# Window attention in blocks of 32 queries with 64x32 float32 score tiles, from the third batch on, before a two-layer feed-forward

## The chip, the cores and the metric

One core of a Trainium2 chip runs the whole program. The metric is the device time of one execution in microseconds (us), as the median of several runs.

## The reference

Eight batches, eight heads, 512 local and 32 global tokens, head dimension 64. Each local query sees the 32 global keys and the local keys at most 32 positions away; each global query sees all 544 keys. The attention output (4352 rows of 512) goes through a feed-forward with 2048 hidden units.

```python
s_g = scale * np.matmul(q_g, k_all.transpose(0, 1, 3, 2))
out_g = np.matmul(sm(s_g), v_all)
s_ll = scale * np.matmul(q_l, k_l.transpose(0, 1, 3, 2))
mask = np.abs(pos[:, None] - pos[None, :]) <= window          # window = 32
s_ll = np.where(mask, s_ll, -1000000000.0)
s_lg = scale * np.matmul(q_l, k_g.transpose(0, 1, 3, 2))
a_l = sm(np.concatenate([s_lg, s_ll], axis=-1))
out_l = np.matmul(a_l, np.concatenate([v_g, v_l], axis=2))
...
h = x @ w_in                                                  # x: 4352 x 512
g = h - np.tanh(h)
return (g @ w_out).astype(np.float32)
```

## The kernel before

**The work.** Heads go in pairs, `Pair(j)`: pairs 0 to 7 are batches 1 and 2, pairs 8 to 31 are batches 3 to 8. A chunk is the feed-forward of one batch. It has 16 steps; a step is 12 hidden matmuls (`add_hidden`, L1521, 128x512) and 12 output matmuls (`add_out`, L1569, 128x512), because weights and activations are each split in a high and a low part (type float32r) and three of the four products are taken. The last batch's chunk and the global rows go through `Tail` (L1914, L1940, L2034).

**Attention of a pair from the third batch on** (`split_attention`): the global scores (L1340, 4 matmuls), and then, for each half `tp` of the 512 queries, scores of two tiles of 128 queries against 224 keys each (`scores`, L1150, float32r, three passes, 12 matmuls for two heads), mask and row maximum on DVE (L1459), exponential on ACT (L1466), scaling on POOL (L1229), 16 transposes of the probabilities back on TensorE (`transposes`, L1171), copies to SBUF, and the product with the values (`add_product`, L1248, float32, 8 matmuls). The first two batches have the same steps with float32 scores (`attention`).

A "visit" (`add_visit`) is a row of such matmul groups that TensorE does without anything between them; it takes all its PSUM banks at its start. A pair has two of them, transposes with the next half's scores (`add_both`), with the products placed on their own.

**PSUM.** Eight banks: attention and hidden matmuls share banks 0 to 3 (`"att"`, `"h"`), the output accumulators take 4 to 7 (`"acc"`). A hidden bank comes free when ACT has taken the tanh (L1529) and DVE the difference (L1532).

**Order.** The order of all instructions is written by a planner in the kernel (`Order.run`) before the program is built: of the operations whose inputs it reckons ready, it takes the one that can start first, and among those that start within `tol` of each other the one with the lowest `due`. `NUDGE` adds a number to the `due` of single operations, `CHOICE` moves single operations between engines. Both are lists of about two thousand and one thousand numbers, found for this very kernel; they begin at operation 214, which is behind the first batch's first steps, and do not touch the tail.

## Time and profile before

| | |
|---|---|
| median of 3 runs | 970.85 us (970.6 to 971.48) |
| the profiled execution | 971.94 us, of which 970.0 us lie between the first and the last instruction (the span) |
| busy: TensorE (PE) | 953.3 us, 98% of the span |
| busy: VectorE (DVE), ScalarE (ACT), GpSimd (POOL) | 645.5, 480.6, 370.7 us |
| granted TensorE clock | 1.000 of 2.4 GHz over the span |
| chain that ended last | PE for 91% of the span |

The table says which engine is filled and that the chain of work that ends last runs on it nearly all the time. A busy time of PE counts a matmul until its modelled end, which overlaps the next matmul; what a group of matmuls costs is read from the start of the group to the start of what follows it. A float32 matmul stands as two records in the trace, a float32r matmul and a transpose as one.

### The profile page before, as it was taken

The numbers are of one execution on the slowest core, as the hardware profiler recorded it, in microseconds if no ns is written. First come the engines' busy times: TensorE is split into PE (matmuls) and PEld (weight loads), VectorE is DVE, ScalarE is ACT, GpSimd is POOL, SyncE is SP. The second block draws the span as 40 slices with busy tenths as digits, with TensorE's granted clock in tenths as the row PEclk, the third lists the DMA queues.
The fourth block names the chain that finished last, engine by engine and source line by source line (L and its number), as shares of the span: only waits on it lengthen the run. The fifth ranks groups of instructions, "written<-read, shape, count | busy, mean of one in ns | idle before, by whom it ended". The sixth has DMA issues, their size and how long they took to land.

```text
span 970.0 us, 18571 instructions
## 1 busy us (share of the span) xinstructions
PE 953.3 (98%) x6411; PEld 782.7 (81%) x6411; DVE 645.5 (67%) x2029; ACT 480.6 (50%) x1332; POOL 370.7 (38%) x512
## 2 busy tenths in 40 slices
PE   7889999999999999999999999999999999999998
PEld 5677777888888888888888888888888888889986
DVE  6997768777666665766666667667635544798773
ACT  6976566646455434563355445534535434433232
POOL 4666756534444532425325343433332343101000
PEclk9999999999999999999999999999999999999999
DMA  8665344322223121321123122221212200100001
GB/s 220 159 180 163 86 118 112 88 39 42 44 47 83 31 41 26 69 65 23 34 39 83 31 41 40 50 71 35 41 20 72 40 2 16 44 1 1 1 1 66
DMA packets 195166, 57.32 MB, mean 59 GB/s; under 512 B 179712, under 2 KB 188416, under 8 KB 195072
## 3 DMA queue, kind: packets, MB, share of 16 engines
q1 hardware_dynamic: 193728, 55.61, 24.3%
q8 instruction: 51, 0.84, 0.4%
q10 hardware_dynamic: 1344, 0.52, 0.2%
q14 instruction: 43, 0.35, 0.1%
HBM read 47.19 MB, written 8.91 MB: 58 GB/s over the span
## 4 chain that ended last, share of the span: by engine, by line
PE 91%; DVE 3%; DMA 1%; POOL 1%; SPq 1%; issue 1%; ACT 1%; ACTq 0%; DVEq 0%; POOLq 0%
PE bank L1569 32%; PE bank L1521 32%; PE bank L1248 6%; PE bank L1914 6%; PE bank L2034 5%; PE bank L1150 4%; PE bank L1171 4%; PE bank L1340 1%; PE bank L1940 1%; DMA wpair<-in_moe_w_out_dram 1%; SPq L1031 0%; POOL prob L1229 0%; DMA stage<-in_moe_w_out_dram 0%; DVE pg L1085 0%; PE bank L1047 0%
## 5 line engine op out<-in xcount | busy, mean ns | idle before, releaser
L1538 POOL TENSOR_TENSOR glo<-t,ghi 128x512 fp32r<-128x512 f32 x89 | 116.6, 1311 | 221.2 <-PE bank L1569 79.6
L1529 ACT ACTIVATE t<-bank 128x512 f32<-128x512 f32 x112 | 66.9, 598 | 199.4 <-PE bank L1521 188.8
L1229 POOL TENSOR_SCALAR prob<-prob,st 128x224 f32<-128x224 f32 x240 | 107.8, 466 | 143.6 <-DVE st L1223 120.1
L1532 DVE TENSOR_TENSOR t<-bank,t 128x512 f32<-128x512 f32 x112 | 77.3, 691 | 124.7 <-ACT t L1529 124.2
L1569 PE MATMUL bank<-w_out_hi,ghi 128*128 128x512 f32 x448 | 125.8, 395 | 0.0
L1569 PE MATMUL bank<-w_out_hi,glo 128*128 128x512 f32 x448 | 124.7, 392 | 0.0
L1569 PE MATMUL bank<-w_out_lo,ghi 128*128 128x512 f32 x448 | 124.5, 392 | 0.0
L1459 DVE CUSTOM_DVE_ANT_0 prob<-bank,mask 128x224 f32<-128x224 f32 x240 | 80.8, 387 | 63.5 <-PE bank L1150 55.9
L1521 PE MATMUL bank<-x_hi,w_in_hi 128*128 128x512 f32 x448 | 123.0, 397 | 0.0
L1466 ACT ACTIVATE prob<-prob,st 128x224 f32<-128x224 f32 x240 | 113.2, 476 | 14.5 <-DVE st L1459 13.3
L1521 PE MATMUL bank<-x_lo,w_in_hi 128*128 128x512 f32 x448 | 120.2, 390 | 0.0
L1521 PE MATMUL bank<-x_hi,w_in_lo 128*128 128x512 f32 x448 | 119.1, 390 | 0.0
L870 ACT COPY keys_first<-bank 128x512 f32<-128x512 f32 (+2 forms) x150 | 69.9, 516 | 87.2 <-PE bank L1171 86.8
L1521 PEld LDWEIGHTS bank<-x_hi,w_in_hi 128*128 128x128 f32 x448 | 81.6, 188 | 21.6 <-issue 3.2
L1521 PEld LDWEIGHTS bank<-x_lo,w_in_hi 128*128 128x128 f32 x448 | 83.8, 188 | 17.7
L1569 PEld LDWEIGHTS bank<-w_out_lo,ghi 128*128 128x128 f32 x448 | 83.0, 188 | 18.4 <-issue 1.0
L1569 PEld LDWEIGHTS bank<-w_out_hi,glo 128*128 128x128 f32 x448 | 83.0, 188 | 18.2 <-issue 0.7
L1521 PEld LDWEIGHTS bank<-x_hi,w_in_lo 128*128 128x128 f32 x448 | 83.6, 188 | 17.3
L1569 PEld LDWEIGHTS bank<-w_out_hi,ghi 128*128 128x128 f32 x448 | 82.3, 188 | 18.7 <-issue 1.4
L1248 PE MATMUL bank<-keys_first,values 128*64 128x160 f32 (+3 forms) x1024 | 68.5, 276 | 4.1 <-ACT keys_first L870 2.9
L1248 PEld LDWEIGHTS bank<-keys_first,values 96*64 96x64 f32 (+1 forms) x1024 | 56.2, 136 | 11.8 <-ACT keys_first L870 6.2
L1382 DVE STREAM_TRANSPOSE gt<-pg 32x128 f32<-32x128 f32 x192 | 53.0, 276 | 10.3 <-POOL pg L1361 4.5
(260 smaller groups left out, 1596.4 us busy)
## 6 DMA issues: line engine op xcount, KB each, us to landing
values<-in_v_l_dram SPq DMA_DIRECT2D x128, 72.0 KB, 2.4
out_dram<-wpair SPq DMA_DIRECT2D x28, 256.0 KB, 2.1
rawkq<-in_k_l_dram SPq DMA_DIRECT2D x96, 64.0 KB, 2.3
rawkq<-in_q_l_dram SPq DMA_DIRECT2D x96, 64.0 KB, 2.3
values<-in_v_g_dram SPq DMA_DIRECT2D x64, 48.0 KB, 2.1
first_q<-in_moe_w_in_dram SPq DMA_DIRECT2D x6, 512.0 KB, 4.4
stage<-in_moe_w_out_dram SPq DMA_DIRECT2D x6, 512.0 KB, 4.6
stage<-in_moe_w_in_dram SPq DMA_DIRECT2D x6, 512.0 KB, 4.4
```

Source lines behind the costliest of these rows:

```text
L870: (nc.scalar.copy if e == "A" else nc.vector.tensor_copy)(dst, src)
L1229: nc.gpsimd.tensor_scalar(x, x, st[:, c:c + 1], 1.0, op0=ALU.mult, op1=ALU.mult)
L1248: nc.tensor.matmul(box["o"][h.e:h.e + D, o0:o0 + c1 - c0], values[:k, h.two, t + t // 2 + a], keys_first[:k, h.two, pair, a, c0:c1], start ...
L1382: nc.vector.transpose(gt[r, :c], view(src, [(P, c), (1, 32)], 32 * q))
L1459: nc.vector.tensor_tensor_reduce(out=self.pt(2 * tp + i)[:, :KC], in0=getattr(self, f"s_{tp}")[:, i, :KC], in1=masks[2 * tp + i], scale=-0 ...
L1466: nc.scalar.activation(x, x, AF.Exp, bias=col[:, c0 + i:c0 + i + 1], scale=-1.0, accum_out=col[:, 8 + tp + c0 + i:9 + tp + c0 + i])
L1521: nc.tensor.matmul(self.h[s][:, j * n:(j + 1) * n], w[:, cc, f * P:(f + 1) * P], self.x()[xi][:, cc, :n], start=part == 0 and cc == 0 and ...
L1529: nc.scalar.activation(tt_[q], self.h[s], AF.Tanh)
L1532: nc.vector.tensor_sub(tt_[q], self.h.pop(s), tt_[q])
L1538: eng[e].tensor_sub(gg[q][1], tt_[q], f32(gg[q][0]))
L1569: nc.tensor.matmul(self.acc[tt], g[:, j * self.n + tt * P:j * self.n + (tt + 1) * P], low_out(f) if wi else high_out(f), start=s == 0 and ...
L1914: nc.tensor.matmul(self.hold(tt, tags), g(), low_out(f) if wi else high_out(f), start=first and k < len(tts), stop=last and k == len(mms) - 1)
```

## The change

From pair 8 on a pair is a `WindowPair`. Each block of 32 queries takes its own 96 local keys and the 32 global ones, so a head's scores are 16 blocks of 32x128, written as 64x32 tiles of the array: 64 contraction rows of one head, 32 columns of one block, two matmuls of 64 moving columns each, in float32 and without the split in parts. The global scores go the same way, in four groups of 32 columns. One visit holds all 64 local and 16 global score matmuls of the pair. The second visit holds the products of the pair before (14 matmuls for each half) and then this pair's 16 transposes. The values are loaded once for each window of 96 keys (14 windows a head). Masks are made anew on POOL for the blocks. `NUDGE` and `CHOICE` are empty; the planner's other numbers stay. The first two batches and the tail keep their code.

```diff
-    NUDGE = {214: 0.47, 215: 39.97, 216: 57.05, 217: 55.56, 218: -51.2, 219: -791.25, 220: -863.76, 221: -648.08,
...
-    CHOICE = {220: {"D": 3.0}, 225: {"A": 1.0}, 226: {"P": 1.0, "D": 0.3}, 231: {"D": 0.3, "A": 1.0}, 237: {"D": 1.0},
...
+    NUDGE = {}
+    CHOICE = {}
...
+    class WindowPair:
+            self.at = base(2 * j) + CFG["win"]
...
+        def scores(self):
+            names = [("s", self.j, h) for h in range(2)]
+            kw, q, g = win_kw, win_q(), self.gcol
+            def mm(e, tags):
+                t_ = self.box["s"] = [bank([P, S], tags[n]) for n in names]
+                for t in range(NT):
+                    for last in range(2):
+                        for i in range(4):
+                            b = 4 * t + i
+                            c = W * window(b) + 2 * W * last
+                            o = t * P + 2 * W * last
+                            for h, x in enumerate(t_):
+                                r = slice(64 * h, 64 * h + 64)
+                                keys = view(kw[r], [(g - c, 2), (1, W)], c) if last else kw[r, c:c + 2 * W]
+                                nc.tensor.matmul(x[W * i:W * i + W, o:o + 2 * W], q[r, W * b:W * b + W], keys,
+                                                 start=True, stop=True, tile_position=(64 * h, W * i), skip_group_check=True)
...
+        def global_scores(self):
+                for x_, n, dims in ((0, 4 * W, [(6 * W, 2), (3 * W, 2), (1, W)]), (1, 2 * W, None)):
+                    for c in range(4):
+                        for h, x in enumerate(t_):
...
+                            nc.tensor.matmul(out, q[r], keys, start=True, stop=True, tile_position=(64 * h, W * c),
+                                             skip_group_check=True)
...
+            def peak(h, tp):
+                def fn(e, _):
+                    for t in (2 * tp, 2 * tp + 1):
+                        c = slice(t * P, t * P + P)
+                        nc.vector.tensor_tensor_reduce(out=self.prob[h][:, c], in0=self.box["s"][h][:, c], in1=win_mask(t), scale=-0.125,
+                                                       scalar=1e30, op0=ALU.add, op1=ALU.min, accum_out=s[:, 4 * h + t:4 * h + t + 1])
...
+        def product(self, half):
+                parts = [(1, 2 * G, 0, 3, W), (2, L + 64, G + 64, 1, 0), (3, L + 96, G + 96, 1, 0), (4, 0, 0, 2, L + 128),
+                         (5, L + 160, G + 160, 1, 0), (6, L + 192, G + 192, 1, 0), (7, G, 0, 2, L + 224 - G)]
...
+                for n, (b, c, o0, k, d) in enumerate(parts):
+                    for h in range(2):
...
+                        nc.tensor.matmul(dst, win_values[h][:, window(b)], src, start=n == 0, stop=n == len(parts) - 1, skip_group_check=True)
...
+        def add_values(self):
+                    nc.sync.dma_start(win_values[h][:96], bass.AP(v.tensor, v.offset, [[D, 96], [W * D, NB - 2], [1, D]]))
+                    nc.sync.dma_start(win_values[h][96:], bass.AP(g.tensor, g.offset, [[D, G], [0, NB - 2], [1, D]]))
...
-    pairs = [Pair(j) for j in range(NH // 2)]
+    pairs = [(Pair if j < H else WindowPair)(j) for j in range(NH // 2)]
...
+    def window_attention(j):
+        p.add_visit(p.at, [p.scores(), p.global_scores()])
+        p.add_softmaxes()
+        p.add_global_softmax()
+        p.add_visit(p.after(9.0), ([] if first else [last.product(0), last.product(1)]) + [p.transposes()])
+        if not first:
+            last.add_outputs()
+        p.add_turned()
+        p.add_values()
```

In `parts` the fourth number k is how many pieces of 32 moving columns a matmul takes: per half four matmuls with 32, two with 64 and one with 96 columns for each head.

On TensorE a pair from the middle of the program stood as follows before. `prob` are the probabilities that are turned, `kw` and `hi` the high parts of keys and queries, `w_out_hi` an output weight; "..." stands for rows of the same group.

```order
L1569 MATMUL bank_104<-w_out_lo,ghi_70 128x512
L1171 MATMUL bank_100<-idr,prob_96 128x64
...
L1150 MATMUL bank_103<-kw,hi_2057 128x224
L1150 MATMUL bank_102<-kw,hi_2057 128x224
...
L1150 MATMUL bank_102<-kw,wraw_2066 128x224
L1248 MATMUL bank_101<-keys_first,values 64x160 x2
L1248 MATMUL bank_101<-keys_first,values 64x96 x4
...
L1248 MATMUL bank_100<-keys_first,values 64x160 x2
L1521 MATMUL bank_102<-x_hi_108,w_in_hi 128x512 x4
```

With the change the same engine's order around one pair is this one: the score visit, feed-forward work, then the product and transpose visit, and feed-forward work up to the next score visit.

```order
L1234 MATMUL bank_102<-w_out_hi,ghi_72 128x512
L867 MATMUL bank_99<-first_m,hi_106 32x64
...
L889 MATMUL bank_101<-first_m,win_gq 32x2x64
...
L1234 MATMUL bank_105<-w_out_lo,ghi_72 128x512
...
L1186 MATMUL bank_99<-x_hi_87,w_in_hi 128x512 x4
...
L1047 MATMUL bank_100<-keys_first,values 64x96
...
L1011 MATMUL bank_99<-idr,prob 128x64
...
L1186 MATMUL bank_99<-x_hi_87,w_in_hi 128x512 x4
...
L867 MATMUL bank_101<-first_m,hi_106 32x64
```

What moved: three stops of TensorE in attention a pair (global scores, transposes with scores and products, transposes with scores) became two. Between the score visit and the next product visit stand 48 feed-forward matmuls at this place, 24 between that one and the next score visit.

On DVE, which frees the score banks and makes the row maxima, the order behind a score visit is now this one (`prob` are the masked scores, `st_93` the statistics, `t_69` a hidden tile, `first_m` the turned keys of the next pair).

```order
L1197 TENSOR_TENSOR t_69<-bank_99,t_69 128x512
L967 ISA prob,st_93<-bank_98,wraw_2020 128x128
...
L901 ISA pg,st_93<-bank_101,wraw_2020 128x192
...
L368 CAST ghi_72<-t_69 128x512
L908 COPY st_93<-st_93 32x2 x3
L918 TENSOR_REDUCE st_93<-st_93 32x2
...
L842 STREAM_TRANSPOSE first_m<-rawkq 128x512
L1197 TENSOR_TENSOR t_68<-bank_98,t_68 128x512
```

Here the eight maxima of both heads and the two of the global scores stand in one piece behind one visit; before, four maxima of 224 columns stood behind each of two visits, and the global ones on their own.

## Rows read from the trace of the kernel before

**Rows 1.** The page: busy us, share and instructions by engine; granted clock in 40 slices.

```profile
PE 953.3 (98%) x6411; PEld 782.7 (81%) x6411; DVE 645.5 (67%) x2029; ACT 480.6 (50%) x1332; POOL 370.7 (38%) x512
...
PEclk9999999999999999999999999999999999999999
```

**Rows 2.** Waits of PE from 60 us to the end: us, times, longest.

```profile
PE bank L1248 <- ACT keys_first L870: 0.3, 1, 0.3
PE bank L1171 <- POOL prob L1229: 0.2, 1, 0.2
```

**Rows 3.** Timeline of PE, one pair of the fifth batch: start, us, group, count.

```profile
502.63 0.42 PE L1340 MATMUL bank<-kw,gq 128*128 128x256 f32 x2
...
503.15 1.08 PE L1521 MATMUL bank<-x_hi,w_in_lo 128*128 128x512 f32 x4
...
508.70 0.69 PE L1171 MATMUL bank<-idr,prob 64*128 64x64 f32 x16
509.20 0.35 PE L1150 MATMUL bank<-kw,hi 64*128 64x224 f32 x2
...
510.12 2.05 PE L1248 MATMUL bank<-keys_first,values 128*64 128x160 f32 x32
512.09 1.20 PE L1521 MATMUL bank<-x_hi,w_in_hi 128*128 128x512 f32 x4
513.12 1.07 PE L1521 MATMUL bank<-x_lo,w_in_hi 128*128 128x512 f32 x4
...
517.66 0.39 PE L1569 MATMUL bank<-w_out_hi,glo 128*128 128x512 f32 x1
517.98 0.69 PE L1171 MATMUL bank<-idr,prob 64*128 64x64 f32 x16
...
519.31 0.50 PE L1569 MATMUL bank<-w_out_hi,ghi 128*128 128x512 f32 x1
519.65 0.40 PE L1569 MATMUL bank<-w_out_lo,ghi 128*128 128x512 f32 x1
```

**Rows 4.** Timeline of PE, eight output matmuls ahead of a visit in the sixth batch.

```profile
667.88 1.07 PE L1569 MATMUL bank<-w_out_hi,glo 128*128 128x512 f32 x4
668.79 1.07 PE L1569 MATMUL bank<-w_out_hi,ghi 128*128 128x512 f32 x4
669.79 0.69 PE L1171 MATMUL bank<-idr,prob 64*128 64x64 f32 x16
```

**Rows 5.** Timeline of PE, float32 matmuls of the second batch (each two records).

```profile
93.54 1.03 PE L1150 MATMUL bank<-first_kw,first_q 64*128 64x224 f32 x8
94.50 0.50 PE L1569 MATMUL bank<-w_out_hi,ghi 128*128 128x512 f32 x1
...
150.89 0.59 PE L1080 MATMUL bank<-first_kw,first_m 128*64 128x256 f32 x2
151.32 0.43 PE L1081 MATMUL bank<-first_kw,first_m 128*64 128x320 f32 x1
```

**Rows 6.** Timeline of PE and list of tile idr, 508.69 to 508.76 us: two first transposes.

```profile
508.70 0.28 PE L1171 MATMUL bank<-idr,prob 64*128 64x64 f32 x2
...
L1171 PE MATMUL bank<-idr,prob x2: 272/272/273, 508.7 to 508.7; 64*128 64x64 f32 x2
```

**Rows 7.** Groups of DVE, ACT, POOL, 250 to 850 us: busy us, mean ns, idle before.

```profile
L1532 DVE TENSOR_TENSOR t<-bank,t 128x512 f32<-128x512 f32 x86 | 59.3, 691 | 103.8 <-ACT t L1529 103.4
L1459 DVE CUSTOM_DVE_ANT_0 prob<-bank,mask 128x224 f32<-128x224 f32 x166 | 55.9, 387 | 54.2 <-PE bank L1150 46.8 <-POOL glo L1538 7.2
...
L1466 ACT ACTIVATE prob<-prob,st 128x224 f32<-128x224 f32 x166 | 78.3, 474 | 12.5 <-DVE st L1459 11.4
L1529 ACT ACTIVATE t<-bank 128x512 f32<-128x512 f32 x86 | 51.4, 598 | 171.9 <-PE bank L1521 163.0 <-POOL prob L1229 8.7
...
L1229 POOL TENSOR_SCALAR prob<-prob,st 128x224 f32<-128x224 f32 x168 | 74.9, 464 | 112.8 <-DVE st L1223 109.9 <-ACT x_hi L870 2.5 <-DVE kw L870 0.4
```

**Rows 8.** The page: DMA issues of local values, KB each, median us to landing.

```profile
values<-in_v_l_dram SPq DMA_DIRECT2D x128, 72.0 KB, 2.4
```

More of the change, by code (lines that the diff above doesn't have):

```diff
@@ L18 @@
 D = 64
+W = 32
 KC = 224
@@ L33, with __init__ @@
 class Later:
-    def __init__(self, pool, shape, tag):
-        self.make = lambda: pool.tile(shape, F32R, name=tag, tag=tag)
+    def __init__(self, pool, shape, tag, dt=F32R):
+        self.make = lambda: pool.tile(shape, dt, name=tag, tag=tag)
         self.tile = None
@@ L80, in add @@
                 before[id(x)] = x
+        if glue is not None:
+            before[id(glue)] = glue
         for x in before.values():
@@ L258 @@
     keys_first = cp.tile([P, 2, 2, 2, 384], F32, name="keys_first", tag="kf")
-    values = cp.tile([P, 2, 6, D], F32, name="values")
+    win_values = cp.tile([P, 960], F32, name="values")
+    values = win_values[:, :12 * D].rearrange("p (a t d) -> p a t d", a=2, d=D)
     SETS = [[f"{n}{u}" for n in ("rk", "rq", "pw", "pk", "pq")] for u in range(2)] + [["raw", "kq", "kw0", "kg0", "hk0"]]
@@ L1688, in attention @@
             p.add_head_scores(tp)
-            if tp and j + 1 == H:
-                next_keys(j)
             p.add_transposes(tp)
             p.add_product(tp)
-    def next_keys(j):
-        if (j + 1) % (H // 2) == 0:
-            add_globals(pairs[j + 1].b)
-        pairs[j + 1].add_split()
-    def split_attention(j):
-        p, more = pairs[j], j + 1 < len(pairs)
-        if j == H:
-            p.add_keys()
-            p.add_head_scores(0)
-        p.add_split_global_scores()
-        for a in p.heads:
-            a.add_values()
-        for h in range(2):
-            p.add_split_global_transpose(h)
-        p.add_both(0, p)
-        if more:
-            next_keys(j)
-            pairs[j + 1].add_keys()
-            p.add_both(1, pairs[j + 1])
-        else:
-            p.add_transposes(1)
-        for tp in range(2):
-            p.add_product(tp)
+    def window_attention(j):
+        p, last = pairs[j], pairs[j - 1]
+        first = last.b < 2
+        if first:
+            add_window_masks()
+        if p.jj == 0:
+            add_globals(p.b)
+        p.add_load()
+        p.add_visit(p.at, [p.scores(), p.global_scores()])
[6 more added lines that the diff above has]
+        p.add_values()
+        for h in range(2):
+            p.add_global_transpose(h)
     chunk = None
@@ L1755 @@
         ffn_steps(chunk, NF, NF + 1)
+    p = pairs[-1]
+    p.add_visit(p.after(32.0), [p.product(0), p.product(1)])
+    p.add_outputs()
     ntail = len(order.ops)
@@ L2186 @@
     for i, x in NUDGE.items():
-        if i < ntail:
-            order.ops[i].due += x
+        order.ops[i].due += x
+    for i, x in HOLD.items():
+        order.ops[i].ready = x
     for i, x in CHOICE.items():
-        for e, pen in x.items() if i < ntail else ():
+        for e, pen in x.items():
             d, old = order.ops[i].eng[e]
```

412 lines of the change are left out of this document (260 added, 152 removed), and 527 rows, old and new, of tables (CHOICE, NUDGE).

## The prediction

> **What bounds the kernel now.** The page's busy shares come first: PE is busy for 98% of the span at the full granted clock (2.4 GHz), the next engine, DVE, for 67% [rows 1]. A busy share can hide waits, so PE's own waits are read next: from 60 us to the end it waited for others twice, 0.5 us in all [rows 2]. The reader is to see that after the first 60 us the time is a sum of PE's work and nothing else. A change that takes work off PE is worth that work, as long as it puts no wait in its place; work taken off DVE, ACT or POOL is worth nothing by itself. In the first 60 us, where PE does wait, the order is the same as before on PE, so I leave that stretch as it is.
>
> **What a pair costs PE now.** I read it from starts in the timeline, not from busy times, since those overlap [rows 3]. The global scores run from 502.63 to 503.15, 0.52 us. The large visit runs from 508.70 to 512.09, 3.39 us. A visit starts late: four feed-forward matmuls take 0.91 us, and from the last four to the visit there are 1.00, so 0.09 us pass [rows 4]. The first four behind it take 1.03 us instead of 0.91, another 0.12. The small visit runs from 517.98 to 519.31, 1.33 us, with 0.32 - 0.23 = 0.09 ahead of it and 0.34 - 0.23 = 0.11 behind it. Sum: 0.52 + 0.09 + 3.39 + 0.12 + 0.09 + 1.33 + 0.11 = 5.65 us a pair. Feed-forward matmuls, first batches and tail do the same work as before.
>
> **The prices of the new matmuls.** A float32 matmul of 256 columns is two records and took 151.32 - 150.89 = 0.43 us [rows 5]: 0.84 ns a column and record. A record of 64 columns is then 0.054 us, one of 128 is 0.107. Two 64-row tiles run side by side: the eight records of 224 columns from 93.54 take 0.96 us until the next group, where one after the other they would need 8 x 0.188 = 1.50, and in pairs 0.75, which leaves 0.21 for lead and end [rows 5]. No row shows eight tiles at once, and that is the open price of this change.
>
> *Score visit.* 64 matmuls are 128 records of 64 columns on eight tiles, 16 on each: 16 x 0.054 = 0.86. The 16 global ones give each tile a matmul of 128 and one of 64 columns: 2 x 0.107 + 2 x 0.054 = 0.32. So 1.18 us if all eight tiles work at once, and with two at a time (9.48 us of records, halved) 4.74. I take 1.18. The two nearest rows speak for it: two row tiles gain their whole factor [rows 5], and the first two transposes, on different tiles, took 0.28 us together where each alone took 0.272 [rows 6]; issue does not hold a second tile back. With 0.09 ahead and 0.21 for lead and end the visit costs 1.48.
>
> *Product visit.* The products now move 704 columns for each head, before 1024 (the counts of the code). The 16 float32 matmuls of before take 512.09 - 510.12 = 1.97 us; at 1.68 ns a column, with the two heads side by side, 1024 columns make 1.72, so 0.25 is lead. Now 704 make 1.18. Eight of a head's fourteen matmuls have only 32 columns, 0.027 a record by columns; whether a record can be that short no row shows. The 16 transposes, eight to each row tile, last 509.20 - 508.70 = 0.50 us, 0.062 each, though 64 columns in one pass would be 0.027 [rows 3]: short records are paced by something else, I think by loading weights. So I count those sixteen records at 0.054, which adds 0.43 (bounds 0 and 0.43, the nearest row says the upper one): 1.61 + 0.25 = 1.86. The transposes are 16 where there were 32: 0.50. With 0.09 and 0.12 around it the visit costs 2.57.
>
> **The sum.** 1.48 + 2.57 = 4.05 a pair, 1.60 less than 5.65. There are 24 such pairs: 38.4 us. The last pair's products stand alone and the first pair's product visit has none, which cancels.
>
> **What else moves, and its cover.** Peaks, exponentials and scaling of a pair now stand behind one visit. Ten maxima at 0.39 at most (they have 128 and 192 columns instead of 224), with the last exponential 0.47 behind, and four of the second head's scalings at 0.46 each, make 3.9 + 0.5 + 1.9 = 6.3 us [rows 7]; statistics and the feed-forward's own work on DVE and POOL come between, say 2 to 3 us more. The cover is what PE does from one visit to the next: 48 feed-forward matmuls at 0.227 are 10.9 us, and the products stand ahead of the transposes, 1.9 us more. So I cost the chain at nothing; without cover it would cost some 9 us a pair. Each visit takes four banks at its start, among them the bank of the hidden step just done, which needs tanh and difference, 0.60 + 0.69 [rows 7]. Ahead of it stand eight output matmuls, 1.81 us. Before, a visit behind exactly that row started 669.79 - 668.79 - 0.91 = 0.09 us late, the same as behind longer ones [rows 4]; nothing was waited for.
>
> The values grow from six to fourteen windows: a transfer of 72 KB landed in 2.4 us [rows 8], the new one has 344 KB. If landing grew with the bytes it would be 11.5 us; from one product visit to the next there are 72 feed-forward matmuls and a score visit, 17.8 us. Behind these loads on SyncE's queue stand the next keys and queries, which are wanted a whole pair later. The masks are built on POOL ahead of the third batch, when it is busy for less than half of the time. All this I cost at nothing.
>
> *Empty tables.* The numbers that had been found took every wait away [rows 2]. The planner alone places a visit as soon as it reckons it ready, and its errors then become waits of PE. Nothing in the profile gives their size; the floor is 0, and a late start as large as the one at each visit now, 0.09 us, is what I allow: 0.1 x 48 visits = 4.8 us. The sum against the profiled execution is 971.94 - 38.4 + 4.8 = 938.3; that execution lies 1.1 above the median of the runs, so the forecast is **937 us**.
>
> **The rivals.**
>
> *Two tiles at a time.* If column tiles do not overlap, the score matmuls cost 4.74 instead of 1.18. A pair then costs 7.61, 1.96 more than before, and 24 of them 47 us more: 971.94 + 47 + 4.8 - 1.1 = 1023. It decides from 2.78 us for the 80 matmuls, that is at fewer than 3.4 tiles at a time. For it: no row shows more than two. Against: the tiles of the products are column tiles of 64, and they do reach 1.97 us where one after the other they would need 3.4 [rows 3]. With four at a time (2.37) the gain is 0.41 a pair, 10 us: 966.
>
> *Records that start one at a time.* The transposes average 0.031 us a record; if that is the pace at which any record starts, 160 of them cost 4.96 instead of 1.18, 2.18 us a pair over before: 971.94 + 52 + 4.8 - 1.1 = 1028. Against it stands the pair that starts together [rows 6]. The Trainium skill, page "TensorE: Matmul & The Clock Gate", section "Wait — 56ns, not 53.3ns?", has such a rule: starts are never closer than about 25 ns, however few columns. By it, as an estimate from that page, 160 records would cost 4.0 us and the kernel end near 1005 us. By that rule two records cannot lie within the 0.28 us row as they do; the trace disagrees wherever tiles differ, which is why this rival gets little.
>
> *The planner's waits eat the gain.* The banks, the row maxima or the values come late at each visit. From 38.4 / 48 = 0.8 us a visit the gain is gone. For it: an order that was searched is replaced by one that was not, and ten maxima now stand on DVE in one piece ahead of the difference that frees a hidden bank. Against it: the cover above, and DVE, ACT and POOL at 67, 50 and 38% with fewer instructions than before. At half that, 0.4 us, the time is 971.94 - 38.4 + 19.2 - 1.1 = 952; at 0.8 it is 971.
>
> **How the numbers follow.** Forecast with its own range: the products by columns alone and no waits give 937 - 10 - 5 = 922; waits of 0.4 a visit give 952. I give that 0.70. Four tiles at a time 0.09 (about 966), waits near 0.8 a visit 0.09 (955 to 985, half of it still faster), two tiles 0.07, one record at a time 0.05. A range from 922 to 967 holds 0.70, less a little for times below it, and most of the 0.09 at 966 and part of the third, some 0.80. A difference under 0.2% cannot be told from none here. Faster 0.82, within that bound 0.03, slower 0.15.
>
> **What would show it.** Right: in the timeline a score visit of 1.4 to 1.6 us from its first score matmul to the feed-forward behind it, a product visit of 2.3 to 2.5, and PE's waits after 60 us below 6 us in all. The page would show PE still at 97 to 98% of a shorter span. Wrong on the tiles: score visits of 2.5 us or more with no wait named. Wrong on the tables: waits of PE for DVE or POOL at the visits' first matmuls, or hidden matmuls that wait for a bank behind the row maxima. What would make it wrong altogether is a lower granted clock in the stretches of small tiles; it stood at full level through the short float32 matmuls of the first 100 us [rows 1].

## The result, and the profile after

The changed kernel takes **954.68 us** (median of 4 runs, 954.18 to 956.09), the kernel before 970.82 in the same comparison: a ratio of 0.9835, 95% interval 0.9818 to 0.9852. That is 16.1 us faster. The sign and the range (922 to 967) hold; the forecast of 937 had promised 34 us, more than twice what came.

The page of the changed kernel: span, busy us with share and instructions by engine, granted clock in 40 slices, and the queue that brings instructions (transfers, MB, share).

```profile
span 952.3 us, 24827 instructions
...
PE 933.9 (98%) x9771; PEld 768.3 (81%) x9771; DVE 554.9 (58%) x1937; ACT 395.8 (42%) x1128; POOL 332.9 (35%) x528
...
PEclk9999999999999999999999999999999999999999
...
q8 instruction: 77, 1.26, 0.6%
```

PE is still the engine that fills the time, at the full granted clock (2.4 GHz), as in [rows 1]; DVE, ACT and POOL have less to do. So the missing gain is PE's own time or its waits. The waits of PE from 60 us to the end (us in total, times, longest):

```profile
PE bank L889 <- issue: 2.1, 2, 1.7
PE bank L1561 <- ACT ghi L368: 1.3, 1, 1.3
PE bank L1186 <- ACT keys_first L368: 0.7, 1, 0.7
PE bank L661 <- POOL prob L719: 0.6, 1, 0.6
PE bank L1186 <- DVE x_hi L368: 0.5, 1, 0.5
PE bank L1234 <- POOL w_out_lo L451: 0.4, 1, 0.4
```

They sum to 5.6 us, before 0.5 [rows 2]; I had allowed 4.8. The largest one has no releaser: "issue" is time in which PE waited for nothing that the profile shows, and it lies at the global scores. The rest must be in the visits. The timeline of PE through one pair of the changed kernel (start, us, group, count), which answers to [rows 3]:

```profile
502.85 1.07 PE L1234 MATMUL bank<-w_out_hi,ghi 128*128 128x512 f32 x4
503.84 0.30 PE L1047 MATMUL bank<-keys_first,values 128*64 128x96 f32 x1
...
505.73 0.71 PE L1011 MATMUL bank<-idr,prob 64*128 64x64 f32 x16
506.37 1.20 PE L1234 MATMUL bank<-w_out_lo,ghi 128*128 128x512 f32 x4
507.40 0.39 PE L1186 MATMUL bank<-x_hi,w_in_hi 128*128 128x512 f32 x1
...
512.16 0.39 PE L1234 MATMUL bank<-w_out_hi,glo 128*128 128x512 f32 x1
512.48 1.43 PE L867 MATMUL bank<-first_m,hi 64*32 64x64 f32 x124
513.69 0.29 PE L889 MATMUL bank<-first_m,win_gq 64*32 64x128 f32 x1
...
514.29 0.50 PE L1234 MATMUL bank<-w_out_hi,ghi 128*128 128x512 f32 x1
514.63 0.40 PE L1234 MATMUL bank<-w_out_lo,ghi 128*128 128x512 f32 x1
```

Read from starts, as before. The product visit: 503.84 to 505.73 products, 1.89; to 506.37 transposes, 0.64; with 0.09 ahead and 1.03 - 0.91 = 0.12 behind it costs 2.74 (forecast 2.57). The score visit: 512.48 to 513.69 scores, 1.21; to 514.29 global scores, 0.60; with 0.32 - 0.23 = 0.09 ahead and 0.34 - 0.23 = 0.11 behind it costs 2.01 (forecast 1.48). A pair costs 4.75, not 4.05, against 5.65 before: 0.90 saved, 21.6 us in 24 pairs. All 24 score visits have 1.21 from the first score to the first global one, so this is a price, not an accident of one pair.

The account closes to within 1 us: 21.6 saved in the visits, 5.1 lost in waits after 60 us, and the first hidden matmul starts at 58.58 us instead of 60.22, 1.6 us that I had not looked for. 971.94 - 21.6 + 5.1 - 1.6 = 953.8; the profiled execution took 954.7.

### The profile page after: what moved, and what is told of

It reads as the page before. It is cut to its first block, busy times and chain, and to the rows that moved or that the text cites. A ratio compares the mean times of both kernels' runs of the same rounds, so it can differ in the third digit from the quotient of the medians.

```text
span 952.3 us, 24827 instructions
## 1 busy us (share of the span) xinstructions
PE 933.9 (98%) x9771; PEld 768.3 (81%) x9771; DVE 554.9 (58%) x1937; ACT 395.8 (42%) x1128; POOL 332.9 (35%) x528
## 3 DMA queue, kind: packets, MB, share of 16 engines
q8 instruction: 77, 1.26, 0.6%
## 4 chain that ended last, share of the span: by engine, by line
PE 91%; DVE 3%; ACT 2%; POOL 1%; DMA 1%; issue 1%; SPq 0%; ACTq 0%; POOLq 0%; DVEq 0%
PE bank L1234 33%; PE bank L1186 31%; PE bank L1561 7%; PE bank L1681 5%; PE bank L1047 5%; PE bank L867 3%; PE bank L1011 2%; PE bank L889 1%; PE bank L1587 1%; DMA wpair<-in_moe_w_out_dram 1%; PE bank L738 1%; PE bank L641 1%; POOL wraw L779 0%; DMA first_raw<-in_q_l_dram 0%; PE bank L661 0%
## 5 line engine op out<-in xcount | busy, mean ns | idle before, releaser
L1203 POOL TENSOR_TENSOR glo<-t,ghi 128x512 fp32r<-128x512 f32 x112 | 145.1, 1295 | 364.4 <-PE bank L1234 317.5
L975 ACT ACTIVATE prob<-prob,st 128x128 f32<-128x128 f32 x192 | 74.8, 391 | 71.4 <-DVE st L967 71.2
L1186 PEld LDWEIGHTS bank<-x_hi,w_in_lo 128*128 128x128 f32 x448 | 83.7, 188 | 17.7 <-issue 0.2
L989 POOL TENSOR_SCALAR prob<-prob,st 128x128 f32<-128x128 f32 x192 | 68.3, 373 | 60.7 <-DVE st L982 48.2
L368 ACT COPY keys_first<-bank 128x512 f32<-128x512 f32 (+1 forms) x106 | 45.0, 488 | 94.8 <-PE bank L1011 81.5
L368 ACT CAST ghi<-t 128x512 fp32r<-128x512 f32 (+1 forms) x76 | 46.4, 610 | 53.9 <-PE bank L1234 32.1
L967 DVE CUSTOM_DVE_ANT_0 prob<-bank,wraw 128x128 f32<-128x128 f32 x192 | 45.7, 283 | 37.2 <-PE bank L867 37.0
L1047 PEld LDWEIGHTS bank<-keys_first,values 128*64 128x64 f32 x672 | 42.1, 138 | 8.5 <-issue 3.9
L1047 PE MATMUL bank<-keys_first,values 128*64 128x32 f32 (+2 forms) x672 | 46.7, 228 | 0.0
```

What stands on the lines that cost most here:

```text
L368: (nc.scalar.copy if e == "A" else nc.vector.tensor_copy)(dst, src)
L967: nc.vector.tensor_tensor_reduce(out=self.prob[h][:, c], in0=self.box["s"][h][:, c], in1=win_mask(t), scale=-0.125, scalar=1e30, op0=ALU.a ...
L975: nc.scalar.activation(x, x, AF.Exp, bias=s[:, k:k + 1], scale=-1.0, accum_out=s[:, 8 + k:9 + k])
L989: nc.gpsimd.tensor_scalar(x, x, s[:, k:k + 1], 1.0, op0=ALU.mult, op1=ALU.mult)
L1047: nc.tensor.matmul(dst, win_values[h][:, window(b)], src, start=n == 0, stop=n == len(parts) - 1, skip_group_check=True)
L1186: nc.tensor.matmul(self.h[s][:, j * n:(j + 1) * n], w[:, cc, f * P:(f + 1) * P], self.x()[xi][:, cc, :n], start=part == 0 and cc == 0 and ...
```

## The experiments

The theory: the score matmuls are paced not by their columns on eight tiles but by their number, and the waits without a name belong to that number too. The rivals: columns on fewer tiles than eight at a time; a fixed cost of entering and leaving a visit; and, for the whole sum, that the emptied tables took the gain.

All runs in one table. "Scores" is the time from the first score matmul to the first global one, "globals" from there to the feed-forward behind it (both the median over the 24 visits), "no name" the waits of PE on "issue" from 60 us to the end, all three from the one execution that was profiled. The times of before in these comparisons were 970.8 to 971.9 us.

| kernel | us | ratio to before (95%) | scores | globals | no name |
|---|---|---|---|---|---|
| changed kernel | 954.68 | 0.9835 (0.9818 to 0.9852) | 1.21 | 0.60 | 2.1 |
| e1: before, tables emptied | 978.99 | 1.0082 (1.0067 to 1.0097) | | | 0 |
| e2: scores of 32 columns | 952.08 | 0.9802 (0.9787 to 0.9817) | 1.06 | 0.56 | 2.4 |
| e3: 32 scores of 128 columns | 942.21 | 0.9704 (0.9689 to 0.9718) | 0.90 | 0.55 | 0 |
| e4: globals, transposes twice | 1000.31 | 1.0296 (1.0271 to 1.0321) | 1.21 | 1.24 | 12.6 |
| e5: half the scores, 16 value transfers | 958.00 | 0.9864 (0.9849 to 0.9879) | 0.90 | 0.55 | 0 |
| e6: globals first | 958.11 | 0.9866 (0.9849 to 0.9882) | 1.48 | 0.36 | 3.6 |
| e7: planner's costs as measured | 954.93 | 0.9835 (0.9820 to 0.9850) | 1.21 | 0.60 | 2.4 |
| e8: half the scores, three copies of keys | 946.52 | 0.9751 (0.9737 to 0.9766) | 0.90 | 0.55 | 0 |
| e9: short products twice | 986.39 (one run) | | 1.21 | 0.60 | 7.8 |
| e10: e8 with e7's costs | 949.12 | 0.9776 (0.9760 to 0.9793) | 0.90 | 0.55 | 0 |
| e11: 16 weight columns | 952.90 (one run) | | 1.17 | 0.59 | 1.6 |
| e12: e8 with 8 global scores | 945.30 | 0.9733 (0.9715 to 0.9750) | 0.90 | 0.51 | 0 |

In e6 "globals" is from the first global score to the first score, and "scores" from there to the feed-forward.

### The tables alone (e1)

```diff
-    NUDGE = {214: 0.47, 215: 39.97, 216: 57.05, 217: 55.56, 218: -51.2, 219: -791.25, 220: -863.76, 221: -648.08,
...
+    NUDGE = {}
+    CHOICE = {}
```

> The kernel before with its order tables emptied and nothing else changed: old attention, the planner's bare order. In the changed kernel PE waits 5.6 us from 60 us to the end, before 0.5. Theory A (the empty tables cost about what those waits show, and the rest of the missing gain lies inside the visits): the time rises by 3 to 8 us, to 974 to 979, and PE's waits after 60 us by the same sum. Rival B (the tables were worth far more with the old attention, and the new attention gains all of the forecast 38 us against that): 985 us or more. Rival C (the tables are worth nothing, the waits of the changed kernel come from its longer chain behind one visit): 970 to 972.

Measured: 978.99, 8.0 us more than before. The size is A's, its mechanism is not: the timeline and the waits of e1 show PE waiting 1.0 us after 60 us, not 8.

```profile
PE bank L722 <- ACT keys_first L344: 0.4, 1, 0.4
PE bank L645 <- POOL prob L703: 0.3, 1, 0.3
PE bank L995 <- DVE x_hi L344: 0.3, 1, 0.3
```

The old attention lost its time in another way. The products, which the found order had put into one visit with transposes and scores [rows 3], now often stand alone, split in two, as here:

```profile
507.98 1.07 PE L1043 MATMUL bank<-w_out_hi,glo 128*128 128x512 f32 x4
508.98 1.10 PE L722 MATMUL bank<-keys_first,values 128*64 128x160 f32 x16
510.01 1.20 PE L1043 MATMUL bank<-w_out_hi,ghi 128*128 128x512 f32 x4
511.04 0.85 PE L995 MATMUL bank<-x_hi,w_in_hi 128*128 128x512 f32 x3
```

Each such stop pays 1.00 - 0.91 = 0.09 ahead and 1.03 - 0.91 = 0.12 behind. Counted in the trace from 215 to 845 us, PE stops 90 times for other work than feed-forward, before 70 times: 20 x 0.21 = 4.2 us, and two halves of the products take 2.11 us on average where one piece took 1.97, 0.14 in each of some 22 pairs, 3.1 us. With 0.5 us more of waits this makes 7.8. So the tables held visits together. In the first 60 us, emptying them gained: the first hidden matmul starts at 58.84 us in e1 and at 60.22 before, so behind it e1 lost 979.10 - 971.94 + 1.4 = 8.5 us between the two profiled executions. In the changed kernel the two visits a pair are fixed in the code (its trace has 47 stops in the same stretch), so this loss cannot occur there; on equal terms, both without tables, the new attention gains 978.99 - 954.68 = 24.3 us.

### What paces the scores (e2, e3, e11)

e2, the same 64 matmuls of half the columns:

```diff
-                                keys = view(kw[r], [(g - c, 2), (1, W)], c) if last else kw[r, c:c + 2 * W]
-                                nc.tensor.matmul(x[W * i:W * i + W, o:o + 2 * W], q[r, W * b:W * b + W], keys,
+                                keys = kw[r, c:c + W]
+                                nc.tensor.matmul(x[W * i:W * i + W, o:o + W], q[r, W * b:W * b + W], keys,
```

> The changed kernel with the same 64 score matmuls a pair, each of 32 columns instead of 64: every second block of 32 keys is left out of the scores. From its first to the first global score a score visit takes 1.21 us now. Theory A (the matmuls are paced by their number, about 16.7 ns each, not by their columns): 1.1 to 1.2 us, and the kernel stays within 3 us of 954.7. Rival B (paced by columns, only with fewer than eight tiles at a time): 0.55 to 0.70 us, and 24 x 0.55 = 13 us are saved, 941. Rival C (a fixed cost of 0.35 on top of columns): 0.75 to 0.85, 945.

e3, half the matmuls of twice the columns:

```diff
-                    for last in range(2):
+                    for last in range(1):
...
-                                keys = view(kw[r], [(g - c, 2), (1, W)], c) if last else kw[r, c:c + 2 * W]
-                                nc.tensor.matmul(x[W * i:W * i + W, o:o + 2 * W], q[r, W * b:W * b + W], keys,
+                                keys = kw[r, c:c + 4 * W]
+                                nc.tensor.matmul(x[W * i:W * i + W, o:o + 4 * W], q[r, W * b:W * b + W], keys,
```

> The changed kernel with 32 score matmuls a pair of 128 columns each instead of 64 of 64: the same columns, half the instructions. The fourth block of keys of each query block is then the next window instead of the global keys. Theory A (number): 32 x 16.7 ns would be 0.53, so the columns decide, 8 rounds of 0.107 = 0.86 and a lead: 0.88 to 0.98 us instead of 1.21, and 24 x 0.27 = 6.5 us less, about 948. Rivals B (columns on fewer tiles than eight at a time) and C (a fixed cost): 1.15 to 1.25 us, and 954 to 956.

e11, half the weights:

```diff
-                                nc.tensor.matmul(x[W * i:W * i + W, o:o + 2 * W], q[r, W * b:W * b + W], keys,
+                                nc.tensor.matmul(x[W * i:W * i + W // 2, o:o + 2 * W], q[r, W * b:W * b + W // 2], keys,
```

> The changed kernel with 16 query columns as weights of each score matmul instead of 32: half of the queries of every block are left out of the scores, the 64 matmuls and their 64 key columns stay. It asks what number means in the pace of 16.7 ns a score matmul. If each instruction has its price, whatever it loads: 1.2 us from the first score to the first global score, as now. If the loading of weights sets the pace, by its columns: 0.9 to 1.0 us, where the key columns take over (0.86 and a lead).  The two waits without a name stay either way, since the instructions do.

The timeline of PE at a score visit, e2:

```profile
462.11 1.26 PE L867 MATMUL bank<-first_m,hi 64*32 64x32 f32 x126
463.17 0.31 PE L889 MATMUL bank<-first_m,win_gq 64*32 64x128 f32 x2
...
463.73 1.19 PE L1234 MATMUL bank<-w_out_lo,ghi 128*128 128x512 f32 x4
```

The same of e3:

```profile
503.92 1.16 PE L867 MATMUL bank<-first_m,hi 64*32 64x128 f32 x64
504.82 0.61 PE L889 MATMUL bank<-first_m,win_gq 64*32 64x128 f32 x32
505.37 0.50 PE L1234 MATMUL bank<-w_out_hi,ghi 128*128 128x512 f32 x1
```

And of e11:

```profile
463.61 1.38 PE L867 MATMUL bank<-first_m,hi 64*16 64x64 f32 x125
464.78 0.29 PE L889 MATMUL bank<-first_m,win_gq 64*32 64x128 f32 x1
```

Half the columns take 1.06 us of 1.21, half the weights 1.17, half the matmuls 0.90. So 64 matmuls take 1.06 even with half their columns, a little under theory A's 1.1 to 1.2; that is 16.6 ns each, and the other half of the columns adds 0.15. The columns rival asked for 0.55 to 0.70 in e2 and the fixed-cost rival for 0.75 to 0.85; both fall, and e3 would have stayed at 1.2 by either. With 32 matmuls the columns take over, and there my price holds: 0.86 was forecast for eight tiles at once, and scores with global scores and the lead take 0.90 + 0.55 = 1.45 where 0.86 + 0.32 + 0.21 = 1.39 stood. e3 as a whole came out 5.8 us under its forecast of 948: the visits save 24 x 0.36 = 8.6 us, not 6.5, and the waits after 60 us are 2.4 us shorter.

One rival would fit these times as well: a floor under each record on its own tile. The transposes have 0.062 us a record on two tiles and the short products of e9 0.061; sixteen records on each tile in 1.06 us are 0.066. The starts of the single records in the traces tell the two apart. With such a floor the eight tiles would start together and then pause. That is how e3 looks, where 128 columns decide: in its first rounds eight records start within 0.05 us, and the next eight 0.11 to 0.13 us after the first of them. In e2, behind the first 32 records and a short pause, two records start every 16 or 17 ns, evenly over the tiles, to the end of the visit. That is one pace for all tiles, and it is 16.7 ns a matmul.

What "number" means: e3 has 24,827 - 21,755 = 3,072 instructions less for 24 x 32 = 768 matmuls less, four for each float32 matmul (two records, two weight loads). 16.6 ns are then 4.2 ns for each, on average; no run prices the four apart. At the head of a visit the pace is quicker: in the first quarter of a microsecond of the visit at 512.48, PE starts 32 of the 128 records, 7.8 ns each, and 10 ns each over the rest (view by stretches, changed kernel, line 867 alone):

```profile
core 0: us, PE busy (x) PEld busy (x), PEclk, DMA share, GB/s
512.48:512.73 0.25, 0.25 (x32) 0.25 (x33) 1.00 0.00 0
```

The Trainium skill, page "TensorE: Matmul & The Clock Gate", section "Wait — 56ns, not 53.3ns?", gives about 25 ns as the least distance of two starts. Here 128 records start within 1.21 us, 9.5 ns on average, so for records on different tiles the trace disagrees.

### The waits without a name (e3, e4, e6, e7)

The longest of them in the changed kernel's timeline:

```profile
272.47 0.55 PE L889 MATMUL bank<-first_m,win_gq 64*32 64x128 f32 x27
274.76 0.21 PE L889 MATMUL bank<-first_m,win_gq 64*32 64x64 f32 x1 [1.75 <-issue]
274.90 1.19 PE L1234 MATMUL bank<-w_out_lo,ghi 128*128 128x512 f32 x4
```

The DMA view of 272 to 276 us (busy share in 40 slices; then queue, packets, MB) has two transfers and nothing else, both of the instruction queue:

```profile
DMA  0800000000000000000000000000000000000070
...
q8 instruction: 2, 0.03, 4.0%
```

e4 issued the global scores and the transposes twice, e6 put the global scores first, e7 changed four of the planner's costs (one of the four is shown):

```diff
+                            for _ in range(2):
+                                nc.tensor.transpose(box[x][:, h, t], self.prob[h][r, t * P:t * P + P], idn[r, r])
...
+                            for _ in range(2):
+                                nc.tensor.matmul(out, q[r], keys, start=True, stop=True, tile_position=(64 * h, W * c),
```

> The changed kernel with each of the 16 global score matmuls and each of the 16 transposes of a visit issued twice, everything else as it is. It gives the slope of both terms: global scores take 0.60 us now, transposes 0.64. If 0.28 of the global scores is lead and end and the rest columns, twice as many take 0.60 + 0.32 = 0.92; if number sets the pace 0.60 + 0.27 = 0.87; if all 0.60 is work, 1.20. If the transposes cost 0.031 each and the rest is the way from one tile shape to the next, twice as many take 0.64 + 0.50 = 1.14; if each one costs 0.04, 1.28. The kernel: 24 x 0.8 = 19 us more, 974, by the first readings; 24 x 1.24 = 30 more, 984, by the last.

```diff
-        p.add_visit(p.at, [p.scores(), p.global_scores()])
+        p.add_visit(p.at, [p.global_scores(), p.scores()])
```

> The changed kernel with the 16 global score matmuls ahead of the 64 scores of a visit instead of behind them; the same instructions. The visit takes 1.21 + 0.60 = 1.81 us now, 0.36 + 0.27 more than 1.18 by columns. Reading A (the scores are paced by number wherever they stand; of the global ones 0.32 are columns and the rest the lead and the end of the visit): 0.35 to 0.45 us from the first global score to the first score, 1.35 to 1.45 from there to the feed-forward, 1.8 in all. Reading B (the global scores are slow in themselves): 0.55 or more for the global ones. Time within 3 us of 954.7 by both; the one or two waits without a name may move.

```diff
-            return dict(fn=mm, d=0.45, names=names, r=["ww", ("gkq", self.b % 2)], res=[f"pg{self.u}{h}" for h in range(2)] + ["pg0", "pg1", "pl0", "pl1"] * (self.j < H + 2),
+            return dict(fn=mm, d=0.6, names=names, r=["ww", ("gkq", self.b % 2)], res=[f"pg{self.u}{h}" for h in range(2)] + ["pg0", "pg1", "pl0", "pl1"] * (self.j < H + 2),
...
```

> The changed kernel with the planner's four costs of the new PE steps set to what the profile shows (scores 1.21, global scores 0.60, transposes 0.64, half a product 0.94 instead of 1.18, 0.45, 0.57, 0.90); no instruction is changed, only their order. If the 5.6 us of waits come from the planner's wrong costs: 950 to 953. If they come from elsewhere (instructions that do not arrive, the tail, the first batches): 954 to 957, with the same waits by name.

A transfer of the instruction queue is 1.26 MB / 77 = 16 KB, and 3,072 instructions less meant 77 - 65 = 12 transfers less in e3: 256 instructions each. A score visit of the changed kernel runs (64 + 16) x 4 = 320 of them in 1.8 us, more than one transfer brings. With 192 a visit (e3) no such wait is left; with 384 (e4) there are eight, 12.6 us. The rows that carry the extremes are e4's

```profile
PE bank L890 <- issue: 12.4, 7, 2.1
```

and e3's list, in which the word does not occur. The count of one visit is not all: e9's score visits have the same 320 as the changed kernel's, and five waits where that one has two.

```profile
PE bank L889 <- issue: 7.8, 5, 2.5
```

The place of the waits says what PE waits for. Counted in the traces over PE's matmuls and weight loads from the first one on, every wait without a name after 60 us, 23 of them in the changed kernel, e2, e4, e6, e7, e9 and e11, begins behind number 256 k + 193 for some whole k: at the same place of a block of 256 each time. It ends 1.3 to 1.6 us after a transfer of the instruction queue has landed (above, at 272.18 + 1.31 = 273.49 for a wait that ends at 274.76), and the block before it had been run in 1.2 to 2.8 us. In e3, e5, e8, e10 and e12, where no visit holds a whole block, the fastest block takes 5.7 us, and there is no such wait. So PE waits for the next block of its instructions. Not every fast block is waited for: the changed kernel has six that run in less than 1.5 us, and behind two of them PE waits; why the other four blocks came in time is open. e11, with the same instructions, shows one such wait where two were expected.

The Trainium skill, page "Runtime: NRT & Kernel Launch", section "Instruction fetch mechanics", has blocks of 16 KiB or 256 instructions and calls the crossing of a block mostly hidden. The trace agrees on both: of 73 crossings after 60 us in the changed kernel two show as a wait without a name, 2.1 us in all.

A long wait can cost more than itself. Three of e4's eight were followed by a stretch in which the granted clock is 0.50, that is 1.2 GHz (192.4 to 195.8, 240.2 to 243.6 and 540.6 to 544.0 us). The first of them, behind a wait that ends at 192.20 (view by stretches, all engines):

```profile
core 0: us, PE busy (x) PEld busy (x) DVE busy (x) ACT busy (x) POOL busy (x), PEclk, DMA share, GB/s
192.40:195.80 3.40, 3.40 (x23) 2.59 (x15) 2.81 (x21) 1.89 (x9) 0.00 (x0) 0.50 0.02 5
```

The other five were not, nor were the changed kernel's two. e4 took 45.6 us more than the changed kernel where 19 or 30 had been forecast: 24 x 1.14 = 27.4 are the doubled work, 10.5 the waits, and by an estimate 5.1 the lower clock (half of 10.2 us); the rest is open.

e7 tells the planner's costs apart from this: 954.93, the same time, with 5.3 us of waits, 2.4 of them without a name. The planner's wrong costs carry nothing that shows.

A visit of e6:

```profile
468.12 0.56 PE L889 MATMUL bank<-first_m,win_gq 64*32 64x128 f32 x32
468.48 1.55 PE L867 MATMUL bank<-first_m,hi 64*32 64x64 f32 x128
469.96 1.20 PE L1186 MATMUL bank<-x_hi,w_in_hi 128*128 128x512 f32 x4
```

e6 has 0.36 us from the first global score to the first score, so 0.32 by columns was right for them and the rest of the 0.60 is the way out of the visit, which the scores pay when they stand last (1.48 instead of 1.21). Reading A held for the global scores; the scores took 1.48 where it had 1.35 to 1.45, and the visit 1.84 in all. The kernel lost 3.4 us, 24 x 0.03 = 0.7 of them in the visit. The waits in the table, 1.5 more, come from an execution of 961.47 us with two stretches at 1.2 GHz (39.9 to 43.4 and 377.9 to 381.3 us); its other three runs took 958.0 to 958.1, so the rest is open.

e4's transposes went from 0.64 to 1.14: sixteen cost 0.50, as before the change. The other 0.14 lies almost wholly behind them: from the start of the last transpose to the feed-forward 0.15 us pass, where before 0.03 passed from it to the scores, which use tiles of the same shape. Its global scores took 1.24, more than either reading with a fixed part gave. Doubled, two matmuls in a row use the same tile; I think that they follow each other there, which was not tried. So this slope says nothing about the single ones; e6 and e12 do.

### The products (e9)

```diff
-                        nc.tensor.matmul(dst, win_values[h][:, window(b)], src, start=n == 0, stop=n == len(parts) - 1, skip_group_check=True)
+                        for again in range(2 if k == 1 else 1):
+                            nc.tensor.matmul(dst, win_values[h][:, window(b)], src, start=n == 0, stop=n == len(parts) - 1 and not again, skip_group_check=True)
```

> The changed kernel with the eight product matmuls of a head that have only 32 columns issued twice (so that these products count twice, which alters the output), everything else as it is. From the first product to the first transpose a visit takes 1.88 us now. It weighs the price I chose for such a matmul, two records of 0.054 us with the two heads side by side: 8 x 2 x 0.054 = 0.86, to 2.74. If a record costs what its columns cost, 0.027: 0.43, to 2.31. The kernel: 23 or 24 such visits, 975 or 965, with more waits without a name by the instructions added.

From the first product to the first transpose 2.87 us in place of 1.88: sixteen more records on each side cost 0.98, 0.061 each. The choice of 0.054 against the columns' 0.027 was right, a little low; the copies follow each other on their tile, which may make them dearer than single ones. Of the 31.7 us more, 23 x 0.98 = 22.6 are this and 5.7 waits without a name. One stretch at 1.2 GHz behind the longest of them (531.1 to 534.5 us) makes 1.7 more by the estimate above; the rest is open.

### The same computation with fewer matmuls (e5, e8, e10, e12)

e3 left the global keys out. To score them in the same matmul they must lie beside each three windows. e5 puts them behind every third window; two of three query blocks then have them between their windows, and the values must be loaded in the same order, in 16 transfers a pair:

```diff
-                nc.vector.transpose(win_kw[:, :S], raw[0])
+                nc.vector.transpose(view(win_kw, [(4 * W, 5), (1, 3 * W)]), view(raw[0], [(3 * W, 5), (1, 3 * W)]))
+                nc.vector.transpose(win_kw[:, 20 * W:21 * W], raw[0][:, 15 * W:])
+                nc.vector.tensor_copy(view(win_kw, [(4 * W, 5), (1, W)], 3 * W), view(win_gk[self.b % 2][:, self.jj], [(0, 5), (1, W)]))
...
+                            nc.tensor.matmul(x[W * i:W * i + W, t * P:t * P + P], q[r, W * b:W * b + W], kw[r, c:c + P],
```

> The changed kernel's own computation with half the score matmuls: the keys are laid out with the global keys behind every third window, so that any four blocks in a row hold three neighbouring windows and the globals, and one matmul of 128 columns scores a query block. It costs a second DVE transpose and a copy of 160 columns a pair, and 16 transfers of values instead of 4. Theory A (number of instructions sets the pace of the score visit, and the two unnamed waits of the global scores belong to it): the score visit is that of the run with half the matmuls, 0.90 us to the first global score and 0.55 to the feed-forward behind it, no wait of PE without a name, 942 to 945. Rival (the added transfers and DVE work end as waits of PE at the product visit): PE waits 5 us or more for values or keys, 947 to 954.

The score visits are those of e3, and yet it takes 958.0. The waits of PE in e5:

```profile
PE bank L1242 <- ACT wpair L368: 4.8, 1, 4.8
PE bank L1050 <- DMA keys_first<-in_v_l_dram: 2.6, 2, 1.6
PE bank L870 <- DVE first_m L848: 1.9, 1, 1.9
```

The rival was right in kind, and the time is above even its 947 to 954. The longest wait is not the one that it named, though: sixteen transfers hold SyncE's queue for 9 us (288.8 to 297.8), the output's transfer stands behind them, its buffer (`wpair`) stays full, and PE's accumulator banks with it. The granted clock is 0.50 from 299.2 to 306.0, at the end of this wait and behind it. e8 keeps the order of the values and writes the keys three times, shifted by a window:

```diff
-                nc.vector.transpose(win_kw[:, :S], raw[0])
+                for dst, first, n in ((win_kw, 0, 5), (win_k1(), 1, 5), (win_k2[0], 2, 2), (win_k2[1](), 8, 1), (win_kw[:, 5 * P:], 11, 1)):
+                    nc.vector.transpose(view(dst, [(P, n), (1, 3 * W)]), view(raw[0], [(3 * W, n), (1, 3 * W)], first * W))
...
+                            nc.tensor.matmul(x[W * i:W * i + W, t * P:t * P + P], q[r, W * b:W * b + W], block_keys(window(b))[r],
```

> The changed kernel's own computation with half the score matmuls, without more transfers of values: the turned keys are written three times, shifted by a window, with the global keys behind every third window, so that one matmul of 128 columns scores a query block. DVE turns 1,344 columns a pair instead of 512, and three or four copies of the globals come on top, some 2 us of DVE or ACT a pair, a pair ahead. Theory A (score matmuls are paced by their number, and the added work lies beside PE): score visits of 0.90 and 0.55 us, no wait of PE without a name, 942 to 945. Rival (any added step ahead of the score visit is late, as with the 16 transfers): PE waits at the first score matmul for the keys, 948 to 956.

946.5 us: the added turns do lie beside PE, DVE being busy 62% of the time. It is 1.5 above the range of A; 2.6 us of waits for the output buffer (`wpair`) are new. e10 gave the planner measured costs once more:

> As the run with three copies of the keys, with the planner's costs of global scores, transposes and products set to the measured 0.55, 0.64 and 0.94. The same instructions in another order: within 3 us of the run with three copies if the planner's costs carry little, as they did in the changed kernel (954.9 against 954.7); lower by 3 or more if they set the remaining waits.

949.1, 2.6 us more, within the bound for "costs carry little" and in the wrong direction. Its waits after 60 us are only 0.6 us longer than e8's. But one of them, 2.0 us for DVE, ends at 405.0, and the clock is low behind it:

```profile
405.50:412.30 6.80, 5.35 (x20) 3.74 (x15) 1.82 (x7) 1.56 (x3) 0.00 (x0) 0.50 1.10 225
```

PE stands for 1.5 of these 6.8 us; half of the other 5.3 is 2.7, as an estimate, which is the whole difference. e12 places the copies so that one matmul gives a tile all its global scores:

```diff
-                for x_, n, dims in ((0, 4 * W, [(8 * W, 2), (4 * W, 2), (1, W)]), (1, 2 * W, None)):
-                    for c in range(4):
...
+                for c in range(4):
+                    for h, x in enumerate(t_):
+                        r = slice(64 * h, 64 * h + 64)
+                        nc.tensor.matmul(x[W * c:W * c + W], q[r], view(kw[r], [(P, 6), (1, W)], W * c), start=True, stop=True,
```

> As the run with three copies of the keys, with the copies placed so that one matmul of 192 columns gives a tile all its global scores: 8 global score matmuls a pair instead of 16, the same columns. DVE has two more small turns a pair. If the 0.55 us that the global scores take there are 0.32 of columns and a fixed lead and end: 0.50 to 0.55 still, and 945 to 947 us, within 2 us of the run with three copies (946.5). If part of it is the number of matmuls: 0.42 or less, and 943 or less.

0.51 us for eight in place of 0.55 for sixteen, so nearly all of it is columns and the way out. **945.3 us** is the shortest time of the runs that compute the whole attention, 0.9733 of before and 9.4 us under the changed kernel.

## Why the prediction was wrong in size

- **What bounds the kernel: right.** PE at 98% and full clock before and after. That work taken off the other engines is worth nothing by itself was not tried.
- **The score visit, "So 1.18 us if all eight tiles work at once ... I take 1.18": this step failed.** Eight tiles do work at once, as e3 shows at 128 columns. But with 64 columns in each record it is the number of matmuls that decides, 16.6 ns each: 64 of them take 1.21 with their columns instead of 0.86. The error was in the argument behind it, "issue does not hold a second tile back" [rows 6]. Two records that start together show how quickly two can start; they do not show at what pace 160 can follow. The number costs 1.81 - 1.45 = 0.36 us a pair. I had left out the 0.11 behind this visit, which I had read off the small visit before, and 0.06 of lead: 0.53 in all, 12.7 us.
- **The product visit: nearly right.** 1.89 against 1.86, the sixteen transposes 0.50 as forecast (e4), and 0.14 more, nearly all on the way from the last transpose to the feed-forward. I had read 0.50 from a row in which scores on tiles of the same shape followed [rows 3], so that way out was missing: with 0.03 for the products 0.17 in all, 4.1 us.
- **The sum.** 4.75 a pair in place of 4.05, 24 x 0.70 = 16.8 us less gain. This is nearly the whole of the miss of 17.7.
- **Empty tables, 4.8 us allowed: right in size, 5.1 more waits than before, but not by my reason.** 2.1 of the 5.6 are waits for instructions (gone in e3 and e8), and better costs for the planner change nothing (e7). What the tables had been worth, 8 us in the old attention, was mostly the holding together of visits, against 1.4 us that they had cost in the first 60 us (e1).
- **The first 60 us: taken as unchanged, 1.6 us shorter.** The premise, the same order on PE, was wrong: the tables reach into this stretch, and from 27 us on the two traces have transposes in another order. e1, which only empties the tables, has its first hidden matmul at 58.84 us, so most of the 1.6 goes with the tables, as far as one execution of each can show.
- **The cover for the chain, the masks, the banks, the values: right.** No wait of PE after 60 us names the row maxima or the values; one of 0.7 us, of a hidden matmul for ACT's copy into `keys_first`, may be a bank. The values landed in 4.2 and 5.3 us where I had feared 11.5 at most.
- **The rivals.** *Two tiles at a time* falls with e3 (its 9.48 us of records are 9.44 by the prices given, which changes nothing). *Records that start one at a time* had the right sort of limit with the wrong pace: 31 ns a record would have been 4.96 us, it was 8.3. *The planner's waits eat the gain* falls: 5.6 us in all.

## What to carry to other kernels

Price many small matmuls twice, by columns over tiles and by number of instructions, and take the larger; here a float32 matmul was four instructions and 16.6 ns, so that on eight tiles its two records had to bring more than 64 columns each before columns decided. The larger of the two is a floor (1.06 us for the scores, measured 1.21), and it is not the only one: on two tiles a record of 32 or 64 columns took 0.061 to 0.062 us on its own tile (e9, the transposes), more than by columns or by number. Count the instructions of a burst too: 192 left no wait without a releaser, 320 left two (e9: five) in 24 visits, and 384 left eight. Read the granted clock behind each long wait, since it fell to half behind some of them. Read the price of a group from a row in which the same kind of work follows it. A row in which two things start together is no evidence for a stream of them; ask for a row with as many as the change has, or keep the whole range open.

## What the runs showed that I had not expected

Half the columns or half the weights hardly change a small float32 matmul's cost (1.06 and 1.17 of 1.21 us for 64), while half the matmuls with the same columns take 0.90. PE can stand for up to 2.5 us (e9) on a wait that names nobody, in a kernel whose instruction queue has 0.6% of the DMA time. And a searched order can be worth 8 us (978.99 against 970.96) with PE's waits at 1.0 us: what it bought was mostly 20 stops fewer, each 0.21 us, and products in one piece, 0.14 us a pair.
